# Sliding-window attention and a gated MLP in one kernel: the last store of the output in two halves on two queues

## The chip, the cores and the metric

The kernel runs on one core of a Trainium2 chip. The metric is the device time of one launch in microseconds. Several launches are timed and their median is given. One further launch is recorded by the hardware profiler, and every row of the profile comes from that one.

The engines go by short names here, as in the profile: PE multiplies matrices, ACT (ScalarE) applies functions and copies, DVE (VectorE) and POOL (GpSimd) work elementwise, and SP (SyncE) only issues transfers and waits. A letter q behind a name (ACTq, SPq) is that engine's instruction sequencer. PEld is PE loading weights.

## The reference

```python
# q, k, v: (4, 8, 768, 64); n_sink = 4, window = 128
scores = (1 / sqrt(D)) * q @ k.transpose(0, 1, 3, 2)
rel = pos[:, None] - pos[None, :]
keep = (pos[None, :] < n_sink) | ((rel >= 0) & (rel < window))
a = softmax(where(keep, scores, -1e9))
x = (a @ v).transpose(0, 2, 1, 3).reshape(3072, 512)
h = x @ w_in                       # w_in: (512, 2048)
g = h * (1 / (1 + exp(-1.702 * h)))
out = g @ w_out                    # w_out: (2048, 512), out: (3072, 512) float32
```

Each token attends to the first four positions of its sequence and to a window of 128 positions. The result, 3072 tokens by 512 features, goes through two matrix products with a gate between them.

## The kernel before

The 3072 tokens are 24 blocks of 128 (`NBLK`), and two blocks at a time make one of 12 groups (`NG`). For each block the attention is computed: loads of q, k and v, transposes, scores, exponentials, the product with v and its normalisation, up to the tile `xn`. A group then goes through the MLP: line 802 multiplies its transposed tokens `xt` by `w_in` into PSUM tiles `mm`, line 832 applies the gate on ACT and writes `gt`, and line 856 multiplies `gt` by `w_out`, sixteen accumulating matmuls for each output tile. The output tile is copied from PSUM to the SBUF tile `osb` (lines 375 to 381, by ACT or DVE), and line 874 stores it to `out_dram` in HBM.

Every output tile is 128 tokens by 512 columns and is stored whole, except the very last one (group 11, second block; `end` is true for it). It is computed in three column parts, as `CFG["last"] = (256, 128, 128)` says: each part has its own sixteen matmuls, its own copy and its own store. So the last store of the kernel is 128 rows by 128 columns of 4 bytes, 64 KB, with 512 bytes in each row.

The order of the work is written out by hand. `SEQUENCE` is a list of words such as `832a`: the number of an operation in the order in which `plan.add` made them, and the letter of the engine that is to issue it (p PE, a ACT, d DVE, t POOL, s SP). `Plan.run` reads nothing else. The numbers that `plan.add` also takes (costs, `xfer`, `post`, `slack`, the keys) are kept with the operation, and this kernel does not use them for the order. A dictionary such as `{SP: 0.5, ACT: 0.5}` says which engines may issue the operation, and `by(e)` picks the queue by the letter.

The end of the list is `831p 821a 827s 832a 833a`. Here 831 is the last quarter of the last part's matmuls, 821 the store of the first part on ACT's queue, 827 the store of the second part on SP's queue, 832 the copy of the last part on ACT, and 833 its store, on ACT's queue.

Each transfer that SP or ACT issues signals its landing on one of eight lanes (semaphores), taken in turn, and before a lane is used again the issuing queue waits until the lane's former transfer has landed. After its last transfer, SP goes through the lanes and waits for each of them. Then the engines meet and the program ends. The profile shows these last waits and the meeting under line 916.

Of the kernel before, what the change touches and what calls it, by code (L numbers as in the profile page):

```python
# [19 lines left out]
P = 128  # L20
# [3 lines left out]
NG = 12  # L24
# [3 lines left out]
PE, ACT, DVE, POOL, SP = "PE", "ACT", "DVE", "POOL", "SP"  # L28
CFG = dict(
    tq=(0, 1, 2, 3, 4, 5, 6, 7),  # L30
    ta=(0, 1, 2, 3, 4, 5),
    tx=(0, 1, 2, 3, 4, 5),
    nb={2: 1, 3: 1},
    wide={1: 'pv', 3: 'pv'},
    fine=(0, 1, 2, 3),
    split=(0, 1),
    gbatch={},
    tanh=(0, 1),
    last=(256, 128, 128),
    hw=['k0'],  # L40
    big=(0, 1, 2, 3),
# [48 lines left out]
775a 764d 766p 767a 776p 777a 780p 781a 782p 462t 754p 788p 463p 755p 464d 789p 477s 783p 647s 756p 765s 709s 784p  # L90
790p 757p 758a 785p 759s 791p 786a 787s 792d 796p 731s 797a 808p 809a 794p 795a 802p 803a 806p 807a 798p 799a 800p
801a 810p 804p 805a 811p 816p 812p 822p 813p 817p 823p 814a 818p 824p 815s 819p 793s 828p 825p 820a 829p 826a 830p
831p 821a 827s 832a 833a
"""


# [69 lines left out]
def kernel(  # L166
# [28 lines left out]
    plan = Plan(RING)  # L195
# [48 lines left out]
    def by(e):  # L244
        return nc.sync if e == SP else nc.scalar
# [24 lines left out]
    ld, qkn = {}, {}  # L270

    def load_block(which, b, key, after=0.0):
        bb, r = divmod(b, 6)
        pair, i = divmod(PLACE[b], 2)
        src = {"q": q, "k": k, "v": v}[which][bb, :, r * P : (r + 1) * P, :].rearrange("h s d -> s h d")
        if which == "v":
            return sw(key, 0.88, lambda b=b, x=2: nc.gpsimd.dma_start(v65[:, b, :, 0:D], src), 0.88 if pair < 4 else 0.95, deps=[z_1], after=after)  # L277
        w = "qk".index(which)
        buf = qkn[pair]
        if which + str(PLACE[b]) in CFG["hw"]:  # L280
            raw = const.tile([P, H * D], FP32, name=f"raw_{which}{b}")
            n = CFG["hw"].index(which + str(PLACE[b]))
            src = {"q": q, "k": k}[which][bb, :, r * P : (r + 1) * P, :].rearrange("h (t e) d -> t h (e d)", e=8)
            got = plan.add(
                {SP: 0.45, ACT: 0.6}, -120 + n, 0, lambda e, src=src, raw=raw, x=9: by(e).dma_start(raw, src), xfer=0.9, post=0.6
            )

            def round16(e, b=b, w=w, i=i):
                dst, src = buf()[:, i, w].rearrange("p h d -> p (h d)"), raw
                if e == ACT:  # L290
                    nc.scalar.copy(out=dst, in_=src)
                else:
                    (nc.vector if e == DVE else nc.gpsimd).tensor_copy(out=dst, in_=src)

            return plan.add({DVE: 0.42, ACT: 0.6, POOL: 0.8}, -110 + n, 0, round16, deps=[got], take=[buf])
        if PLACE[b] in CFG["big"]:
            return sw(
                key, 0.56,
                lambda b=b, w=w, i=i: nc.gpsimd.dma_start(
                    buf()[:, i, w].rearrange("p h d -> p (h d)"),  # L300
                    {"q": q, "k": k}["qk"[w]][bb, :, r * P : (r + 1) * P, :].rearrange("h (t e) d -> t h (e d)", e=8),
                ),
                0.7, take=[buf], after=after,
            )
        return sw(
            key, 0.88, lambda b=b, w=w, i=i: nc.gpsimd.dma_start(buf()[:, i, w], src), 0.88 if pair < 4 else 0.95,  # L306
            take=[buf], after=after,
        )
# [84 lines left out]
    for p, b in enumerate(ORDER):  # L393
# [8 lines left out]
        if p in CFG["tq"]:  # L402
            tps = [ps(t, (P, 4, P), FP16, f"tq{b}_{w}") for w, t in enumerate(CFG["tqb"][p])] if p in CFG["tqb"] else []
            tps = tps or [ps("mm", (P, 8, P), FP16, f"tq{b}")] * 2
            if p in CFG["big"]:
                tps = [
                    ps(t, (P, 4, P), FP32, f"tq{b}_{w}")
                    for w, t in enumerate(CFG["tqb"].get(p, ("mm", "mm")))
                ]

            def tp(w, tps=tps):
                return tps[w]()[:, 4 * w : 4 * w + 4] if tps[0] is tps[1] else tps[w]()

            def t_qk(w, g=g, i=i, p=p, tp=tp):
                src = qkn[g]()[:, i, w].rearrange("p h d -> p (h d)")
                if p in CFG["big"]:
                    dst = tp(w).rearrange("p c t -> p (c t)")
                    for e in range(8):
                        for a in range(2):
                            nc.tensor.matmul(  # L420
                                dst[64 * a : 64 * a + 64, 64 * e : 64 * e + 64],
                                src[:, 64 * e : 64 * e + 64],
                                ident.rearrange("p (t c a) -> p t c a", a=2, t=16)[:, :, :, a], start=True, stop=True,
                            )
                    return
                for c in range(4):
                    nc.tensor.transpose(tp(w)[:, c], src[:, bass.ts(c, P)], ident)

            def copy_qk(e, w, b=b, p=p, tp=tp):
                dst, src = qk_of(b)[:, 4 * w : 4 * w + 4], tp(w)  # L430
                if p in CFG["big"]:
                    dst, src = (
                        dst.rearrange("p c (t e) -> p c t e", e=8),
                        src.rearrange("p x y -> p (x y)").rearrange("p (e t c) -> p c t e", c=4, t=16),
                    )
                copy(e, dst, src)

            parts = []
            for w in range(2):
                a = plan.add(  # L440
                    PE, K0 - 48 + w, 0.43 if p in CFG["big"] else 0.24, lambda w=w, f=t_qk: f(w), deps=[ld["qk"[w] + str(b)], o_const],
                    take=[tps[w]], give=[qkn[g]],
                )
                parts.append(
                    plan.add(
                        {DVE: 0.6 if p in CFG["big"] else 0.34, ACT: 0.5}, K0 - 48 + w, 0,
                        lambda e, b=b, w=w, f=copy_qk: f(e, w),
                        deps=[a], take=[qkt[g]], give=[tps[w]],
                    )
                )  # L450
            o_qkt[b] = parts
        elif i == 0:

            def t_qk(g=g):
                nc.sync.dma_start_transpose(
                    qkt[g]().rearrange("p i c t -> p (i c) t"), qkn[g]().rearrange("p i w h d -> p (i w h d)")
                )

            o_qkt[b] = o_qkt[ORDER[p + 1]] = [
                plan.add(  # L460
                    SP, K0 - 48, 1.75, t_qk, deps=[ld[f"{w}{n}"] for w in "qk" for n in ORDER[p : p + 2]], take=[qkt[g]],
                    give=[qkn[g]], xfer=2.56, post=0.75,
                )
            ]
# [22 lines left out]
        def uniq(bufs):  # L487
            return list(dict.fromkeys(bufs))
# [20 lines left out]
        if r == 0:  # L509
            s_msk = plan.add(  # L510
                PE, K0 - 41, 0.45, lambda own=half, f=masks: f(own), deps=[o_const] + (o_qkt[b] if p else []), take=uniq(owns),
                slack=slack["s"],
            )
            s_own = plan.add(
                PE, K0 - 40, 0.46, lambda b=b, own=half, f=scores: f(own, b),
                deps=o_qkt[b] + [s_msk], give=[qkt[g]], use=uniq(owns),
            )
        else:

            def both(b=b, own=half, prv=prv, f=scores):  # L520
                f(own, b)
                f(lambda lo, hi: prv()[:, lo:hi], b - 1)

            s_own = plan.add(
                PE, K0 - 40, 0.57, both, deps=o_qkt[b] + o_qkt[b - 1], take=uniq(owns) + [prv],
                give=[qkt[g]] + ([qkt[PLACE[b - 1] // 2]] if PLACE[b - 1] // 2 != g else []),
                slack=slack["s"],
            )

            def sinks(b=b, bb=bb, snk=snk):  # L530
                for j in range(4):
                    nc.tensor.matmul(snk()[:, j], qk_of(b)[:, j], ksb[:, bb, j], start=True, stop=True)  # L532

            s_snk = plan.add(PE, K0 - 40, 0.1, sinks, deps=([s_own] if p >= CFG['steady'] else []) + o_qkt[b] + [o_ks[bb]], take=[snk], give=[qkt[g]], slack=slack["s"])
# [252 lines left out]
    for g in range(NG):  # L787
# [53 lines left out]
        for t in range(2):  # L841
# [4 lines left out]
            for part, width in enumerate(CFG["last"] if end else (d_model,)):  # L846
# [5 lines left out]
                for n in range(4):  # L852
# [16 lines left out]
                    ),  # L869
                    deps=[prev], take=[osb], give=[po],  # L870
                )
                plan.add(
                    {SP: 0.5, ACT: 0.5} if end else SP, 16 * g + 12 + 4 * t, 0.5,
                    lambda e=SP, row=row, osb=osb, cols=cols: by(e).dma_start(out[row : row + P, cols], osb()[:, cols]),
                    deps=[ev], give=[osb], xfer=0.72 * share, post=2.0 if g >= NG - 3 else 1.0,
                )

    order = plan.run()
    with tc.manual_schedule():
# [41 lines left out]
```

## Time and profile before

| | us |
|---|---|
| median of three runs | 227.18 |
| the three runs | 227.09, 227.18, 228.92 |
| the profiled run, as timed | 228.16 |
| span of the profiled run | 226.5 |
| PE busy in it | 214.0 (94%) |

The span runs from the first to the last instruction that the profile has. The profiled run took 1.7 us more than its span, which lie outside of what the profile shows. Its granted TensorE clock was 1.00. The profile's lines are shown in the prediction, where they are used.

### The profile page before, as it was taken

The numbers are of one execution on the slowest core, as the hardware profiler recorded it, in microseconds if no ns is written. First come the engines' busy times: TensorE is split into PE (matmuls) and PEld (weight loads), VectorE is DVE, ScalarE is ACT, GpSimd is POOL, SyncE is SP. The second block draws the span as 40 slices with busy tenths as digits, with TensorE's granted clock in tenths as the row PEclk, the third lists the DMA queues.
The fourth block names the chain that finished last, engine by engine and source line by source line (L and its number), as shares of the span: only waits on it lengthen the run. The fifth ranks groups of instructions, "written<-read, shape, count | busy, mean of one in ns | idle before, by whom it ended". The sixth has DMA issues, their size and how long they took to land.

```text
span 226.5 us, 5648 instructions
## 1 busy us (share of the span) xinstructions
PE 214.0 (94%) x2378; PEld 151.9 (67%) x2378; DVE 133.3 (59%) x238; ACT 141.6 (63%) x201; POOL 113.9 (50%) x137
## 2 busy tenths in 40 slices
PE   1977999999999999999999999999999999999994
PEld 1557876776784686684695685697764777754864
DVE  1898988689678782782886677466477371110100
ACT  2487786768859848348247559767694766812622
POOL 8592756869990399860893480763405230210000
PEclk9999999999999999999999999999999999999999
DMA  6999999999999999999999999399967620206303
GB/s 131 166 204 193 177 189 195 156 129 160 140 149 158 255 169 138 146 123 187 285 145 138 227 112 151 59 228 96 225 98 139 92 56 3 52 0 206 121 0 139
DMA packets 123512, 32.47 MB, mean 143 GB/s; under 512 B 114880, under 2 KB 120416, under 8 KB 123488
## 3 DMA queue, kind: packets, MB, share of 16 engines
q0 software_dynamic: 71792, 13.51, 74.2%
q1 hardware_dynamic: 51408, 18.42, 39.8%
q8 instruction: 18, 0.29, 0.5%
q10 hardware_dynamic: 288, 0.20, 0.3%
q14 instruction: 6, 0.05, 0.1%
HBM read 27.46 MB, written 6.29 MB: 149 GB/s over the span
## 4 chain that ended last, share of the span: by engine, by line
PE 69%; DMA 20%; POOL 5%; DVE 2%; issue 1%; SPq 1%; ACT 0%; POOLq 0%
PE mm L856 30%; PE mm L802 28%; DMA qkn<-in_q_dram 7%; DMA w_in<-in_moe_w_in_dram 4%; DMA qkt<-qkn 3%; DMA at<-a 3%; PE own L503 2%; POOL qkn L306 2%; PE av L741 2%; PE av L737 2%; PE av L731 2%; DMA consts<-cconst 2%; PE prv L503 1%; DVE e L600 1%; POOL at L646 1%
## 5 line engine op out<-in xcount | busy, mean ns | idle before, releaser
L802 PE MATMUL mm<-xt,w_in 128*128 128x256 f16 (+1 forms) x896 | 93.8, 257 | 1.8 <-DMA w_in<-in_moe_w_in_dram 1.4
L856 PE MATMUL mm<-w_out,gt 128*128 128x512 f16 (+2 forms) x416 | 91.9, 363 | 0.0
L802 PEld LDWEIGHTS <-w_in 128*128 128x128 f16 x896 | 75.2, 98 | 14.4 <-DMA w_in<-in_moe_w_in_dram 1.8
L832 ACT ACTIVATE gt<-mm 128x512 f16<-128x512 f32 x88 | 51.0, 596 | 47.4 <-PE mm L802 47.0
L856 PEld LDWEIGHTS <-gt 128*128 128x128 f16 x416 | 37.2, 98 | 32.1
L642 POOL TENSOR_SCALAR_AFFINE_SELECT atp<-at 128x1024 f16<-128x1024 f16 (+1 forms) x22 | 22.3, 1014 | 69.3 <-DMA at<-a 65.5
L549 DVE COPY_PREDICATED own<-consts,prv 128x1024 f32<-128x1024 uint16 x20 | 24.6, 1228 | 24.8 <-PE prv L503 24.8
L559 DVE TENSOR_REDUCE mx<-own 128x8 f32<-128x1024 f32 (+1 forms) x28 | 29.8, 1069 | 1.5 <-PE own L503 0.7
L600 DVE TENSOR_TENSOR e<-own,mx 128x1024 f32<-128x1024 f32 (+1 forms) x26 | 28.4, 1094 | 0.6
L639 ACT ACTIVATE a<-e 128x1056 f16<-128x1056 f32 (+1 forms) x26 | 25.0, 979 | 1.9 <-DVE e L624 1.3
L646 POOL TENSOR_SCALAR_AFFINE_SELECT at<-at 128x1024 f16<-128x1024 f16 (+1 forms) x22 | 22.5, 1024 | 1.5
L277 POOL DMA_DIRECT2D v<-in_v_dram x24 | 21.6, 906 | 1.9 <-DMA w_out<-in_moe_w_out_dram 1.9
L381 ACT COPY osb<-mm 128x512 f32<-128x512 f32 (+2 forms) x16 | 8.4, 531 | 18.8 <-PE mm L856 15.7
L306 POOL DMA_DIRECT2D qkn<-in_q_dram x20 | 17.9, 901 | 3.4 <-DMA w_in<-in_moe_w_in_dram 1.8
L832 ACT ACT_TABLE_LOAD x15 | 19.2, 1283 | 0.3
L306 POOL DMA_DIRECT2D qkn<-in_k_dram x20 | 17.8, 902 | 2.4 <-PE snk L532 1.6
L639 ACT ACT_TABLE_LOAD x14 | 18.0, 1283 | 0.2
L749 DVE TENSOR_TENSOR xn<-av,rcp 128x512 f16<-128x512 f32 (+1 forms) x25 | 16.0, 638 | 0.9
L737 PE MATMUL av<-v,at 128*128 128x65 f16 x180 | 16.1, 194 | 0.1
L748 DVE RECIPROCAL rcp<-av 128x8 f32<-128x8 f32 (+1 forms) x25 | 5.0, 199 | 18.7 <-PE av L741 18.5
L737 PEld LDWEIGHTS <-at 128*128 128x128 f16 x192 | 14.1, 97 | 2.6 <-ACT at L381 0.7
L377 DVE COPY osb<-mm 128x512 f32<-128x512 f32 x8 | 5.5, 690 | 16.8 <-PE mm L856 16.4
(67 smaller groups left out, 174.6 us busy)
## 6 DMA issues: line engine op xcount, KB each, us to landing
out_dram<-osb SPq DMA_DIRECT2D x23, 256.0 KB, 2.6
qkn<-in_q_dram POOLq DMA_DIRECT2D x24, 128.0 KB, 5.4
v<-in_v_dram POOLq DMA_DIRECT2D x24, 128.0 KB, 5.2
qkn<-in_k_dram POOLq DMA_DIRECT2D x23, 128.0 KB, 6.5
w_in<-in_moe_w_in_dram POOLq DMA_DIRECT2D x4, 512.0 KB, 9.9
w_out<-in_moe_w_out_dram POOLq DMA_DIRECT2D x4, 512.0 KB, 11.4
at<-a SPq DMA_TRANSPOSE x18, 3.5
raw_k<-in_k_dram SPq DMA_DIRECT2D x1, 256.0 KB
```

The costliest lines, as they stand in the source:

```text
L277: return sw(key, 0.88, lambda b=b, x=2: nc.gpsimd.dma_start(v65[:, b, :, 0:D], src), 0.88 if pair < 4 else 0.95, deps=[z_1], after=after)
L306: key, 0.88, lambda b=b, w=w, i=i: nc.gpsimd.dma_start(buf()[:, i, w], src), 0.88 if pair < 4 else 0.95,
L549: nc.vector.copy_predicated(out=own(lo, hi).rearrange("p l j s -> p (l j) s"), mask=later.unsqueeze(1).to_broadcast((P, 4 * (hi - lo), P)) ...
L559: lambda lo=lo, hi=hi, own=half, small=small: nc.vector.tensor_reduce(out=small[:, lo:hi], in_=own(lo, hi), axis=AX.X, op=ALU.max),
L600: nc.vector.tensor_tensor(out=e32()[:, 512 * lo : 512 * hi].rearrange("p (l j s) -> p l j s", j=4, s=P), in0=own(lo, hi), in1=small[:, lo: ...
L639: nc.scalar.activation(out=a16()[:, lo:hi], in_=e32()[:, lo:hi], func=AF.Exp, scale=scale)
L642: nc.gpsimd.affine_select(out=atp()[:, lo : lo + n], in_=at()[:, lo : lo + n], pattern=[[0, n], [-1, P]], compare_op=ALU.is_gt, fill=0.0, ...
L646: nc.gpsimd.affine_select(out=at()[:, lo : lo + n], in_=at()[:, lo : lo + n], pattern=[[0, n], [1, P]], compare_op=ALU.is_ge, fill=0.0, ba ...
L737: nc.tensor.matmul(acc[:, j], at()[:, c], v65[:, b, h], start=(r == 0), stop=(r == 0))
L802: nc.tensor.matmul(ht()[:, n], w_in16[:, c, bass.ts(f, P)], xt[g]()[:, tok, c], start=(c == 0), stop=(c == 3))
L832: lambda fs=fs, cols=cols, gt=gt, ht=ht: nc.scalar.activation(out=gt()[:, fs[0] : fs[-1] + 1, cols], in_=ht(), func=AF.Gelu_apprx_sigmoid),
L856: nc.tensor.matmul(po(), gt()[:, F, bass.ts(t, P)], w_out16[:, F, cols], start=(F == 0), stop=(F == NF - 1))
```

## The change

The store of the last part, and no other, is made in two: `pieces` is 2 for the last part of the last tile. The first piece takes rows 0 to 63 of `osb`, the second rows 64 to 127, each with the same 128 columns. Both depend on the same copy (832). The first keeps number 833 and ACT's queue; the second is the new operation 834, with the letter s, so SP issues it. All other words of `SEQUENCE` are the same.

The diff also alters four numbers that `plan.add` keeps with operations (a `post`, two costs of PE steps, and POOL as an engine that could do one rounding step). The written order does not read them.

```diff
-831p 821a 827s 832a 833a
+831p 821a 827s 832a 833a 834s
...
-                {SP: 0.45, ACT: 0.6}, -120 + n, 0, lambda e, src=src, raw=raw, x=9: by(e).dma_start(raw, src), xfer=0.9, post=0.6
+                {SP: 0.45, ACT: 0.6}, -120 + n, 0, lambda e, src=src, raw=raw, x=9: by(e).dma_start(raw, src), xfer=0.9, post=1.25
...
-            return plan.add({DVE: 0.42, ACT: 0.6, POOL: 0.8}, -110 + n, 0, round16, deps=[got], take=[buf])
+            return plan.add({DVE: 0.42, ACT: 0.6}, -110 + n, 0, round16, deps=[got], take=[buf])
...
-                    PE, K0 - 48 + w, 0.43 if p in CFG["big"] else 0.24, lambda w=w, f=t_qk: f(w), deps=[ld["qk"[w] + str(b)], o_const],
+                    PE, K0 - 48 + w, 0.40 if p in CFG["big"] else 0.24, lambda w=w, f=t_qk: f(w), deps=[ld["qk"[w] + str(b)], o_const],
...
-                PE, K0 - 40, 0.57, both, deps=o_qkt[b] + o_qkt[b - 1], take=uniq(owns) + [prv],
+                PE, K0 - 40, 0.65, both, deps=o_qkt[b] + o_qkt[b - 1], take=uniq(owns) + [prv],
...
-                plan.add(
-                    {SP: 0.5, ACT: 0.5} if end else SP, 16 * g + 12 + 4 * t, 0.5,
-                    lambda e=SP, row=row, osb=osb, cols=cols: by(e).dma_start(out[row : row + P, cols], osb()[:, cols]),
-                    deps=[ev], give=[osb], xfer=0.72 * share, post=2.0 if g >= NG - 3 else 1.0,
-                )
+                pieces = 2 if end and part == len(CFG["last"]) - 1 else 1
+                for piece in range(pieces):
+                    at_rows = slice(piece * P // pieces, (piece + 1) * P // pieces)
+                    plan.add(
+                        {SP: 0.5, ACT: 0.5} if end else SP, 16 * g + 12 + 4 * t, 0.5,
+                        lambda e=SP, row=row, osb=osb, cols=cols, rows=at_rows: by(e).dma_start(
+                            out[row + rows.start : row + rows.stop, cols], osb()[rows, cols]
+                        ),
+                        deps=[ev], give=[osb], xfer=0.72 * share / pieces, post=2.0 if g >= NG - 3 else 1.0,
+                    )
```

## The prediction

> **What bounds the kernel now.** I read the page's first part and its chain first, then the end of the chain, and then, since the change touches only the end, the timeline, the transfers and the waits of the last three microseconds.
>
> ```profile
> span 226.5 us, 5648 instructions
> PE 214.0 (94%) x2378; PEld 151.9 (67%) x2378; DVE 133.3 (59%) x238; ACT 141.6 (63%) x201; POOL 113.9 (50%) x137
> PE 69%; DMA 20%; POOL 5%; DVE 2%; issue 1%; SPq 1%; ACT 0%; POOLq 0%
> ```
>
> PE is busy for 94% of the span and carries 69% of the chain that ends last. The 20% of DMA in it are loads and transposes, and the change touches none of them. So the body of the kernel stays as it is, and the question is what happens behind the last matmul. The chain, asked from 217 us on, has this:
>
> ```profile
> 217.26 6.14 PE mm L856 x60
> 223.40 0.02 issue
> 223.42 0.27 ACT osb L381
> ```
>
> The chain ends with the last copy, at 223.42 + 0.27 = 223.69. The span ends at 226.5. The 2.8 us between them are the last store and what waits for it, and they have to be read from other views. The timeline of the two queues:
>
> ```profile
> 222.76 0.37 ACTq L874 DMA_DIRECT2D out_dram<-osb  x1
> 223.42 0.27 ACT L381 COPY osb<-mm 128x128 f32<-128x128 f32 x1 [0.40 <-PE mm L856]
> 223.72 0.34 ACTq L874 DMA_DIRECT2D out_dram<-osb  x1
> ...
> 223.05 0.33 SPq L874 DMA_DIRECT2D out_dram<-osb  x1
> ```
>
> ACT issues the last store 0.03 behind the copy, and the issue takes 0.34, to 224.06. SP issued its own last store at 223.05 and was done with that at 223.38, so it stands free 0.31 before the last copy ends. What the transfer engines then do, in 40 slices of 25 ns from 224.4 to 225.4:
>
> ```profile
> DMA  0000000547999996521000000000000000000000
> GB/s 0 0 0 0 0 0 20 164 143 246 307 348 348 348 246 185 144 62 41 21 0 0 0 0 0 0 0 0 0 0 0 0 0 0 0 0 0 0 0 0
> DMA packets 144, 0.07 MB, mean 66 GB/s; under 512 B 16, under 2 KB 144, under 8 KB 144
> q10 hardware_dynamic: 144, 0.07, 22.3%
> ```
>
> These 144 packets are the last store: 128 rows and 16 small ones, on ACT's queue (q10). The first move in the seventh slice, at 224.55, and the last in the twentieth, at 224.90. The first lie 224.55 - 223.72 = 0.83 behind the start of the issue. The 16 engines were busy for 22.3% of 1 us, which is 0.22 each, spread over 0.35 because they do not all begin together. Then the landing, from the waits of SP's queue on line 916 between 225.2 and 225.6:
>
> ```profile
> L916 SPq EVENT_SEMAPHORE  x5: 28/28/28, 225.3 to 225.6; - x5
> ...
> SPq L916 <- DMA out_dram<-osb: 0.5, 1, 0.5
> ```
>
> SP saw the last store landed at 225.3, which is 0.4 behind its last packet. Four more checks of lanes take it to 225.6, about 0.07 each, and the remaining 0.9 to the end of the span are the engines' meeting. So of the 2.8 us behind the copy, 0.83 go until packets move, 0.35 are movement, 0.4 the way from the last packet to the signal, and 1.2 the closing of the program. The change can shorten or lengthen the second of these, and the first for one half of the rows. The other terms do not depend on how the bytes are divided.
>
> **The change part by part.** The instruction lists of the two builds differ in this: ACT's last store is 64x128 in place of 128x128, SP has one store of 64x128 more at its end (69 rows in place of 68), and the line numbers behind it are shifted. The four altered numbers of the planner leave every list as it was, so their cost is nothing, and there is no cover that could go.
>
> *ACT's store with 64 rows.* Does its issue get shorter with fewer rows? The nearest rows:
>
> ```profile
> L250 SPq DMA_DIRECT2D ownm<-cown x1: 391/391/391, 41.3 to 41.3; - x1
> ...
> L874 ACTq DMA_DIRECT2D out_dram<-osb x2: 343/355/367, 222.8 to 223.7; - x2
> ```
>
> A transfer with 32 rows took 0.39 to issue and those with 128 rows 0.34 and 0.37. The issue does not follow the number of rows, so I take 0.34 for 64 rows too, and 0.83 until its first packet.
>
> *SP's new store.* It waits for the same copy. SP's queue is free 0.31 before, so it issues beside ACT, at about 223.72, and takes the 0.33 of its former store: nothing is added to the path by the issue itself. It needs a lane again, so SP first checks that lane's former transfer. By the instruction list that is the store of an earlier tile, issued in the stretch from 208 to 214, and the packets of that stretch were through by 211.4:
>
> ```profile
> DMA  0000000299992399999999300000000000000000
> out_dram<-osb SPq DMA_DIRECT2D x3, 256.0 KB, 4.5
> ```
>
> The slices here are of 0.15. The three stores in it landed, at the median, 4.5 after their issue, which is by 214, ten microseconds early. The check falls into SP's free time. Queued behind the new store on SP are its closing waits, and all engines wait for these. They begin at about 224.06 in place of 223.38. How much room they have:
>
> ```profile
> SPq L916 <- DMA out_dram<-osb: 1.7, 4, 0.6
> ```
>
> SP stood waiting for landings for 1.7 us in all in these closing waits. Until 225.3 it needs only a few checks of 0.07 each, so the 0.68 of delay lies inside these 1.7. If the cover were gone, it would cost up to 0.68.
>
> *The transfer.* The bytes are the same. A second transfer adds at most another 16 small packets. Two queues now feed the engines, each with half the rows. From below: the engines cannot do the work in less than the 0.22 that they were busy, so at the best 0.35 - 0.22 = 0.13 is won, if both halves begin together and the uneven start closes. From above: SP's half begins behind ACT's by a whole issue, 0.33. Then its packets begin at 224.55 + 0.33 = 224.88 and need half of 0.22 and the same spread of 0.13, to 225.12, which is 0.22 later than 224.90 (an estimate from these rows). Between -0.13 and +0.22 I take 0.0: both queues begin 0.83 behind an issue that starts at the same time, the bytes are the same and I assume that the engines share them as before, and the unevenness of the start (0.13), which belongs to how the engines are set off and not to the bytes, probably stays.
>
> A rule of the Trainium skill speaks against the change. The page "DMA: Bandwidth & Descriptors", section "Rules for kernel authors", says of two transfers to disjoint partition halves: don't bother, they serialize, because both halves use the same 16 engines. By it the lower bound falls away and the sum is 0.0 with no -0.13 beside it. The row with 22.3% agrees that the engines are the common part, and it leaves the 0.13 open.
>
> *The sum.* Span 226.5 + 0 (issue) + 0 (closing waits) + 0.0 (transfer, -0.13 to +0.22) = 226.5. The profiled run took 228.16, 1.7 more than its span. The median of the three runs is 227.18, and the same sum on it gives 227.2.
>
> **The rivals.** *One issue at a time.* ACT's and SP's issues use something in common, and the second waits for the first. Against it: SP's row at 223.05 began while ACT's (222.76 + 0.37 = 223.13) still ran. They overlapped by 0.08, and SP's took 0.33, no longer than the ACT issue that ran alone (0.34). For it: 0.08 of 0.33 is a small overlap, and the change makes it complete. The time: +0.22 as worked out, 227.4. It decides once SP's packets begin later than ACT's by more than the 0.11 of busy time that a half takes.
>
> The Trainium skill has this as a rule: "Perfetto Trace Analysis", section "DMA Instruction — HWDGE (DVE, Sync)", says that the block which makes the descriptors is shared between the issuing sequencers and is locked for exclusive use by one instruction. The time by it is the +0.22 above. The overlap of 0.08 without a longer issue speaks against a lock over the whole issue, not against one over a part of it.
>
> *The even start.* Two queues set the engines off more evenly and the 0.13 is won: 227.05. For it: the digits rise over five slices before they reach 9. Against it: the same digits would rise so if the engines are started one after the other whatever the queue.
>
> *A slow landing.* SP's half, as the second of two stores in flight, lands as late as the three stores from 208 to 214, 4.5 after its issue. Then SP sees it at 223.72 + 4.5 = 228.2 in place of 225.3, +2.9, and the median would be 230.1. It passes 1% (2.27 us) if that landing takes more than 1.6 + 2.27 = 3.9, where the last store of before had 1.6:
>
> ```profile
> DMA to landing us min/median/max: 1.6/1.6/1.6
> ```
>
> Against it: those three were of 256 KB each, and here are two of 32 KB. The two stores that were in flight together at the end of before had landed by the same closing waits, none of which lasted over 0.6.
>
> That the change does not do what it says is ruled out by the lists.
>
> **How the numbers follow.** The forecast, no change to speak of (within 0.1), has 0.60; one issue at a time 0.22; the even start 0.14; the slow landing 0.02; 0.02 is left for a measurement that strays. The time is that of the likeliest, 227.2. About 1% is what a measurement of this kernel can tell from no change. Nothing here reaches a gain of 1%, so faster gets 0.01 for a stray measurement. Slower gets 0.03, from the slow landing and the other half of the stray ones. Within 1% is left with 0.96. The cases reach from 227.05 to 227.4. The runs themselves scatter more: 227.09 to 228.92, with the profiled one at 228.16, so a median of a few runs can well come out as high as 228.2. Downwards I take the lowest run less the 0.13, 226.96, and 0.3 below it, since three runs show the lower end only roughly. The range is 226.7 to 228.2.
>
> **What would show it.** In the profile after, two issues of line 877 should begin within 0.05 of each other, some 0.03 behind the last copy, each about 0.33 long. If SP's takes 0.5 or more, the issues go one at a time. The two queues' packets (q10 and q1, 80 each at most) should both begin about 0.83 behind the issues and end about 0.35 later; an end at 0.22 shows the even start. The last landing should stand 1.6 behind the issue, and 1.2 should follow until the end of the span. PE's busy time and the chain up to the last copy should be those of before. I am wrong if the part from the copy's end to the end of the span is not 2.8 within 0.2, or if the body of the kernel moves although no instruction in it changed.

## The result, and the profile after

| | before | after |
|---|---|---|
| median of 22 runs | 227.76 us | 228.49 us |
| lowest and highest | 226.86, 228.92 | 227.55, 229.82 |
| ratio after to before | | 1.0032 (95% interval 1.0017 to 1.0046) |
| the profiled run, as timed | 228.16 us | 228.24 us |

The changed kernel is slower by 0.3%, which is 0.7 us (0.4 to 1.05 by the interval). The kernel before came out at 227.76 over 22 runs, where the three runs shown at first had 227.18.

The page and the end of the chain of waits, after:

```profile
span 226.5 us, 5650 instructions
PE 213.9 (94%) x2378; PEld 151.9 (67%) x2378; DVE 133.0 (59%) x238; ACT 141.5 (62%) x201; POOL 113.9 (50%) x137
...
216.84 6.14 PE mm L856 x60
222.97 0.02 issue
223.00 0.27 ACT osb L381
```

The span is 226.5 as before, and it would be wrong to read from that that nothing happened. The last copy ends at 223.27 where it ended at 223.69 before. The body of this execution was 0.4 shorter, and the end took back as much. The body scatters: over the executions recorded in this study, all with the same instructions up to the last copy or nearly so, the last copy began between 222.2 and 225.5. Against this, the distance from the last copy's end to the end of the span is almost fixed for one kernel. It is called the tail from here on, and is taken from the trace's time stamps, which are in nanoseconds: 2.77 before, 3.26 after. The tail grew by 0.49.

Where, is seen in the last issues of the two queues (the timeline, asked for each engine by itself), in the transfers from 224.4 to 225.4 in slices of 25 ns, and in SP's waits:

```profile
223.00 0.27 ACT L381 COPY osb<-mm 128x128 f32<-128x128 f32 x1 [0.40 <-PE mm L856]
223.29 0.55 ACTq L877 DMA_DIRECT2D out_dram<-osb  x1
...
223.29 0.56 SPq L877 DMA_DIRECT2D out_dram<-osb  x1
```

```profile
DMA  0000235798999974421000000000000000000000
GB/s 0 0 0 0 82 82 143 205 266 246 307 308 267 247 185 103 103 42 21 20 0 0 0 0 0 0 0 0 0 0 0 0 0 0 0 0 0 0 0 0
DMA packets 160, 0.07 MB, mean 66 GB/s; under 512 B 32, under 2 KB 160, under 8 KB 160
q10 hardware_dynamic: 80, 0.03, 12.3%
q1 hardware_dynamic: 80, 0.03, 11.7%
```

```profile
L921 SPq EVENT_SEMAPHORE  x5: 28/28/28, 225.3 to 225.6; - x5
...
SPq L921 <- DMA out_dram<-osb: 0.9, 1, 0.9
```

The two issues begin together, as intended, but each takes 0.55 in place of 0.34. The first packet moves at 224.50, 1.21 behind the issue in place of 0.85 (the prediction read 0.83 from slices of 25 ns; by the time stamps it is 0.85). The movement takes 0.4. SP's last long wait, for ACT's landing, is 0.9 in place of 0.5, and the landing of its own half lets it pass 0.17 after that. By the time stamps the tail's growth divides into 0.37 until ACT's first packet, 0.06 in the movement and 0.12 between the last packet and SP's seeing it. After the landing SP goes through one lane fewer, which takes 0.07 off.

### The profile page after: what moved, and what is told of

The parts are those of the page before. It is cut to its first block, busy times and chain, and to the rows that moved or that the text cites. A ratio compares the mean times of both kernels' runs of the same rounds, so it can differ in the third digit from the quotient of the medians.

```text
span 226.5 us, 5650 instructions
## 1 busy us (share of the span) xinstructions
PE 213.9 (94%) x2378; PEld 151.9 (67%) x2378; DVE 133.0 (59%) x238; ACT 141.5 (62%) x201; POOL 113.9 (50%) x137
## 4 chain that ended last, share of the span: by engine, by line
PE 86%; DMA 10%; DVE 1%; issue 0%; SPq 0%; POOL 0%; ACT 0%
PE mm L856 37%; PE mm L802 35%; DMA qkn<-in_q_dram 4%; DMA w_in<-in_moe_w_in_dram 4%; PE own L503 3%; PE av L741 2%; PE av L737 2%; PE av L731 2%; PE prv L503 2%; DMA consts<-cconst 2%; PE snk L532 1%; PE mm L427 1%; DVE e L600 1%; DVE mx L559 1%; PE mm L679 1%; PE own L495 0%
```

## The experiments

The end of every execution is read in the same way. All times in this table are in us, from the trace's time stamps. "Lag" is from the start of the issue to the first packet, "landing" from the last packet to SP's passing its wait for the last landing. Where two stores end the kernel, ACT's stands first.

| kernel | last stores | issue | lag | landing | tail |
|---|---|---|---|---|---|
| before | 128 rows | 0.34 | 0.85 | 0.41 | 2.77 |
| after | 64 rows and 64 rows | 0.55, 0.56 | 1.21, 1.28 | 0.53 | 3.26 |
| after, once more | the same | 0.55, 0.56 | 1.21, 1.27 | 0.53 | 3.27 |
| half of the rows alone | 64 rows | 0.53 | 1.19 | 0.36 | 3.03 |
| half of the columns alone | 128 short rows | 0.34 | 0.85 | 0.38 | 2.67 |
| column halves | 128 and 128 short rows | 0.37, 0.33 | 0.94, 0.83 | 0.55 | 2.95 |
| 96 and 32 rows | 96 rows and 32 rows | 0.38, 0.34 | 0.89, 0.84 | 0.43 | 2.83 |

**One half alone.** Is it the second issue that makes the first slow, or the form of the store? The most direct test keeps ACT's half and drops SP's.

```diff
-831p 821a 827s 832a 833a 834s
+831p 821a 827s 832a 833a
...
-                for piece in range(pieces):
+                for piece in range(1):
```

> Rows 64 to 127 of the last part are not stored; ACT stores rows 0 to 63 alone. Theory A (two issues at the same time hinder each other): with no issue beside it, ACT's takes 0.34 again, not 0.55, its packets begin 0.85 behind its start, and the end of the span comes 2.7 to 2.8 behind the last copy, as before the change. Theory B (a store of 64 rows is slow by itself): ACT's issue takes 0.55 although it is alone, and the end comes 3.2 behind the copy. Theory C (the cost is a second landing to wait for): 0.55 for the issue remains, but the end comes 0.1 to 0.2 earlier than after the change, as SP's later landing is gone.

```profile
223.35 0.27 ACT L381 COPY osb<-mm 128x128 f32<-128x128 f32 x1 [0.40 <-PE mm L856]
223.65 0.53 ACTq L877 DMA_DIRECT2D out_dram<-osb  x1
```

With nothing beside it, the issue of 64 rows still takes 0.53. Theory A has fallen for the issue, theory B holds for it. But the tail is 3.03, between the 2.77 of before and the 3.26 of the change, so something is left that the second store brings: 0.23, where theory C had said 0.1 to 0.2. The time was 1.0007 of the kernel before (0.9975 to 1.0038), which does not tell 0.26 us from none.

**Both halves on ACT's queue.**

```diff
-831p 821a 827s 832a 833a 834s
+831p 821a 827s 832a 833a 834a
```

> Both halves are issued by ACT, one behind the other. Theory A: the issues cannot overlap, so each takes about 0.34, the second begins 0.38 behind the first, its packets begin 0.85 behind that, and the end comes about 2.8 + 0.38 - 0.1 = 3.1 behind the copy, near the 3.2 of the change although only one queue is used. Theory B: each takes 0.55, and the end comes about 3.6 behind the copy. Theory C: each 0.34, and the end 3.1 or later, because two landings are waited for.

```profile
L877 ACTq DMA_DIRECT2D out_dram<-osb x2: 522/568/614, 225.8 to 226.3; - x2
```

The issues took 0.52 and 0.61, one behind the other, and the tail was 3.61: theory B's numbers. The landing of the second was seen 0.37 behind its last packet, as for a store alone. The ratio was 1.0094 (1.0057 to 1.0131) from four runs, more than the 0.84 us in the tail account for (0.4%). The last copy of its profiled run ended 2.1 us later than in before and 2.5 later than in after. Why these four were slower is not settled.

**The halves one after the other on two queues.** The last copy is cut in two as well, and ACT stores the first half before it copies the second.

```diff
-831p 821a 827s 832a 833a 834s
+831p 821a 827s 832a 833a 834a 835s
...
+                for piece in range(2 if last else 1):
+                    at_rows = slice(64 * piece, 64 * piece + 64) if last else slice(0, P)
...
-                        e, osb()[:, cols], po(), 0.5 if x in CFG["tanh"] else 1.0
+                            e, osb()[rows, cols], po()[rows], 0.5 if x in CFG["tanh"] else 1.0
```

> The last copy is made in two halves of 64 rows with ACT's store of the first between them, so SP issues the second half about 0.65 behind ACT. Theory A: no overlap, both issues take 0.33 to 0.34, and SP's packets begin 0.85 behind its issue; from the second copy's end to the end of the span 2.7 to 2.8, the amount from before. Theory B: both issues take 0.55, and the end comes 3.1 or later behind the second copy. Theory C: issues of 0.34, the first half has long landed, and the end comes 2.8 behind the second copy; together with the single store this would leave A and C to be told apart by the issue times in the other runs.

```profile
222.76 0.53 ACTq L877 DMA_DIRECT2D out_dram<-osb  x1
223.33 0.26 ACT L381 COPY osb<-mm 64x128 f32<-64x128 f32 x1 [0.60 <-ACT osb L381]
...
223.62 0.56 SPq L877 DMA_DIRECT2D out_dram<-osb  x1
```

No overlap, and still 0.53 on ACT and 0.56 on SP: the form is slow on either queue. From the second copy's end to the end of the span it took 2.99, near the 3.03 of a half alone (theory B had said 3.1 or later). The time was 1.0056 of the kernel before (1.0038 to 1.0073): the whole copy would have ended 0.86 earlier, and with the 0.22 of the longer tail that makes 1.08 us, 0.5%.

**Halves by columns.** The same two queues at the same time and the same bytes, but all 128 rows in each store.

```diff
-                    at_rows = slice(piece * P // pieces, (piece + 1) * P // pieces)
+                    at_rows = slice(0, P)
+                    step = (whole.stop - whole.start) // pieces
+                    cols = slice(whole.start + piece * step, whole.start + (piece + 1) * step)
```

> The last part is split by columns in place of rows: 128 rows of 256 bytes on each of ACT's and SP's queues at the same time. Theory A with a price for each row (the queues share the making of descriptors): twice the rows of the change, so each issue takes about 0.34 + 0.44 = 0.78, and the end comes 3.6 or later behind the copy. Theory A with a price for each transfer: 0.55 each as in the change, and the end about 3.3 behind the copy. Theory B (64 rows are slow): 0.34 each, since the rows are 128, and the end 2.8 behind the copy. Theory C: 0.55 or less each, and the end 3.0 to 3.2.

```profile
L880 SPq DMA_DIRECT2D out_dram<-osb x1: 332/332/332, 222.5 to 222.5; - x1
L880 ACTq DMA_DIRECT2D out_dram<-osb x1: 365/365/365, 222.5 to 222.5; - x1
```

Two issues that begin 4 ns apart take 0.33 and 0.37. So a simultaneous issue makes an issue 0.03 longer at most, and the 0.2 of the change belongs to 64 rows. ACT's first packet does come 0.09 later beside another issue (0.94 in place of 0.85), so a small part may be shared. The tail was 2.95 and not the 2.8 that theory B alone gave. The ratio was 1.0005 (0.9977 to 1.0034).

**Half of the columns alone** gives the fourth corner: the same edit, made on the kernel with the column halves.

```diff
-831p 821a 827s 832a 833a 834s
+831p 821a 827s 832a 833a
...
-                for piece in range(pieces):
+                for piece in range(1):
```

> Columns 64 to 127 of the last part are not stored; ACT stores the other 64 columns, 128 rows of 256 bytes, alone. It is the fourth corner beside the single half of 64 rows (3.0 from the copy's end to the end of the span), the pair of those (3.3) and the pair of column halves (2.9). If a pair costs 0.2 whatever its form, the end comes 2.7 behind the copy, and the packets begin 0.85 behind the issue in place of 0.94. If the pair of column halves costs nothing by itself, it comes 2.9 behind.

```profile
224.50 0.27 ACT L381 COPY osb<-mm 128x128 f32<-128x128 f32 x1 [0.40 <-PE mm L856]
224.80 0.34 ACTq L880 DMA_DIRECT2D out_dram<-osb  x1
```

The tail was 2.67. The four corners now add up. From the whole store to half its bytes: 2.77 to 2.67, 0.1 won. From 128 short rows to 64 long ones: 2.67 to 3.03, 0.36 lost. From one such store to two: 3.03 to 3.26, 0.23 lost; by columns 2.67 to 2.95, 0.28 lost. The larger part of the second store's price is in the landing: in the pairs SP saw the last landing 0.53 and 0.55 behind the last packet, in the single stores 0.36 and 0.38, a difference of 0.17 each time. Another 0.13 (rows) and 0.11 (columns) passes before the last packet. With the row halves SP then goes through one lane fewer, which takes 0.07 off.

**Which numbers of rows are slow?** A ladder of stores in SP's idle time, in the kernel before: parts of a tile that is already stored are stored again, one behind the other.

```diff
+LADDER = ((0, 128, 0, 128), (0, 64, 128, 256), (0, 96, 256, 384), (64, 96, 128, 256), (96, 112, 128, 256), (64, 128, 384, 512), (0, 64, 384, 512), (96, 128, 256, 384))
...
+    for lo, hi, left, right in LADDER:
+        plan.add(
+            SP, 900, 0.5,
+            lambda row=row, osb=osb, lo=lo, hi=hi, cols=slice(left, right): nc.sync.dma_start(
+                out[row + lo : row + hi, cols], osb()[lo:hi, cols]
+            ),
+            deps=[stored], give=[osb],
+        )
```

> The kernel before, with eight more stores on SP's queue in its idle time before the last tile's: parts of a tile that is already stored are stored again, of 128, 64, 96, 32, 16, 64, 64 and 32 rows of 512 bytes, one behind the other. Stores one behind the other took 0.42 to 0.46 to issue with 128 rows in the trace of before. Theory D1 (any number of rows other than 128 takes a slower way, a fixed 0.18 more): all but the first take 0.60 to 0.65. Theory D2 (the price grows as the rows get fewer): 96 rows 0.50, 64 rows 0.62, 32 rows 0.7, 16 rows 0.75. Theory D3 (a form that the queue has not just had costs once): each change of form 0.6, the second of the two neighbouring stores of 64 rows 0.44. The time stays that of before.

In their order, the issues took 0.33 (128 rows), 0.57 (64), 0.57 (96), 0.42 (32), 0.42 (16), 0.52 (64), 0.59 (64) and 0.58 (32). None of the three theories gives this row: 32 rows come out both ways. What it leaves open is whether a store was slow by itself or because of the one ahead of it on the queue. So the next two kernels let each store of such a ladder wait for the landing of the one before, by making them overlap.

```diff
-LADDER = ((0, 128, 0, 128), (0, 64, 128, 256), (0, 96, 256, 384), (64, 96, 128, 256), (96, 112, 128, 256), (64, 128, 384, 512), (0, 64, 384, 512), (96, 128, 256, 384))
+LADDER = ((0, 64, 0, 128), (0, 32, 0, 128), (0, 96, 0, 128), (0, 128, 0, 128))
...
+LADDER = ((0, 16, 0, 128), (0, 112, 0, 128), (64, 128, 0, 512), (0, 128, 0, 512))
```

> The kernel before, with four more stores in SP's idle time, of parts of a tile that is already stored: 64, 32, 96 and 128 rows of 512 bytes. They overlap, so each waits for the landing of the one before and is issued alone, as the last store of the kernel is. Theory D1 (any number other than 128 is slow): 0.53, 0.53, 0.53 and 0.33. Theory D2 (fewer rows, slower): 32 rows above 64, 64 above 96, 128 at 0.33. Theory D4 (64 and 96 rows are slow, few rows are not, as the ladder has it but for its last store): 0.53, 0.33, 0.50 and 0.33. The packets of 64 rows begin 1.2 behind the issue, those of 128 rows 0.85. As in the kernel with four more stores, the end comes 2.5 behind the last copy.

> The same with 16 rows and 112 rows of 512 bytes, 64 rows of 2048 bytes and 128 rows of 2048 bytes. D1: 0.53, 0.53, 0.53 and 0.33. D2: 16 rows slowest, 112 near 0.36. D4: 0.33, 0.50, 0.53 and 0.33. If the length of a row decides as well, the 64 rows of 2048 bytes differ from the 0.53 that 64 rows of 512 bytes took. End 2.5 behind the last copy.

The timeline of SP's queue, one row asked for each store (64, 32, 96 and 128 rows in the first kernel; 16, 112, 64 and 128 in the second):

```profile
213.44 0.57 SPq L885 DMA_DIRECT2D out_dram<-osb  x1
215.35 0.35 SPq L885 DMA_DIRECT2D out_dram<-osb  x1
216.78 0.32 SPq L885 DMA_DIRECT2D out_dram<-osb  x1
218.30 0.35 SPq L885 DMA_DIRECT2D out_dram<-osb  x1
```

```profile
214.94 0.34 SPq L885 DMA_DIRECT2D out_dram<-osb  x1
216.37 0.32 SPq L885 DMA_DIRECT2D out_dram<-osb  x1
217.93 0.57 SPq L885 DMA_DIRECT2D out_dram<-osb  x1
220.27 0.36 SPq L885 DMA_DIRECT2D out_dram<-osb  x1
```

Only 64 rows are slow: 0.57, with rows of 512 bytes and of 2048, in the lower and in the upper half, first in the row or third. 16, 32, 96, 112 and 128 rows take 0.32 to 0.36. The lags agree: 1.22 for both stores of 64 rows, 0.82 to 0.86 for all others. Theories D1, D2 and D4 have all fallen. The ladder is explained with it: the stores of 96 and 32 rows that took 0.57 and 0.58 stood right behind one of 64 rows, the two of 32 and 16 rows that took 0.42 did not. What stands right ahead on the queue matters for 128 rows too: in the kernel before, SP's stores of 128 rows took 0.57 to 0.65 right behind a transposing transfer (`DMA_TRANSPOSE`), 0.42 to 0.46 right behind another plain transfer, and else 0.33 to 0.38. So only issues made with nothing right ahead can be compared.

**The change with another cut.** If this is the cause, the change loses most of its price when one number in it is altered.

```diff
-                    at_rows = slice(piece * P // pieces, (piece + 1) * P // pieces)
+                    at_rows = slice((0, 96)[piece], (96, 128)[piece]) if pieces == 2 else slice(0, P)
```

> The change with one number altered: ACT stores rows 0 to 95 and SP rows 96 to 127, both at the same time, in place of 64 and 64. Theory E (64 rows, and only they, cost 0.2 in the issue and 0.35 until the first packet; two stores that end together cost 0.25 more whatever their form): both issues 0.32 to 0.37, first packets 0.82 to 0.95 behind them, and the end 2.9 to 3.0 behind the last copy, between the 2.8 of before and the 3.3 of the change; the time is 0.1% above the kernel before, which five rounds may not tell from none. Theory D1 (any number but 128 is slow): issues of 0.53 and the end at 3.2 to 3.3. If two stores cost nothing once neither has 64 rows, the end is at 2.8 or earlier.

```profile
L877 SPq DMA_DIRECT2D out_dram<-osb x1: 343/343/343, 224.7 to 224.7; - x1
L877 ACTq DMA_DIRECT2D out_dram<-osb x1: 375/375/375, 224.7 to 224.7; - x1
```

The issues are back at 0.34 and 0.38, and the tail is 2.83, a little better than the 2.9 to 3.0 expected. The second store costs less here, and the landing is 0.43: SP's 32 rows were through 0.16 before ACT's 96, where the two equal halves ended within 0.03 of each other, and the column halves within 0.12. The ratio to the kernel before was 1.0014 (0.9991 to 1.0038).

**The change once more.**

> The changed kernel once more, for a second reading of its end on this chip. If the end's lengthening is the form of the store and not chance: both issues 0.55 to 0.57, the first packets 1.2 behind them, and the end 3.2 to 3.3 behind the last copy. If it was chance, one of the three is back at 0.34, 0.85 or 2.8.

Issues of 0.55 and 0.56, lags of 1.21 and 1.27, a tail of 3.27, and a ratio of 1.0033 (1.0008 to 1.0058). It was not chance.

**A shorter tail.** Reading the closing waits suggested another thing. SP goes through its eight lanes in a fixed order, and behind the last store's lane four more stood. With four more transfers ahead of it, the last store takes the last lane. First by four redundant stores in SP's idle time (the ladder with four times 128 rows), then without redundancy, by issuing an earlier tile's store in five parts by columns.

```diff
+LADDER = ((0, 128, 0, 128), (0, 128, 128, 256), (0, 128, 256, 384), (0, 128, 384, 512))
```

> The kernel before, with four more stores of 128 rows in SP's idle time, so that the last store's lane is the last that SP checks. In the trace of before four more checks of 0.06 each followed the landing of the last store. If these stand on the path, the end comes 0.24 earlier: 2.5 behind the last copy in place of 2.8, and the time would be 0.1% below the kernel before, about what five rounds can just tell or not. If they do not, 2.8.

```diff
-                    lambda e=SP, row=row, osb=osb, cols=cols: by(e).dma_start(out[row : row + P, cols], osb()[:, cols]),
+                    lambda e=SP, row=row, osb=osb, cols=slice(0, 256) if five else cols: by(e).dma_start(
+                        out[row : row + P, cols], osb()[:, cols]
+                    ),
...
+    for left in range(256, 512, 64):
+        plan.add(
+            SP, 900, 0.5,
+            lambda row=row, osb=osb, cols=slice(left, left + 64): nc.sync.dma_start(out[row : row + P, cols], osb()[:, cols]),
+            deps=[ev], give=[osb],
+        )
```

> The kernel before, with the store of one earlier tile, in SP's idle time, issued in five parts by columns (256 and four times 64, always 128 rows), so that no byte is stored twice and the last store's lane is the last one checked. If the order of the checks is the cause of the earlier end in the kernel with four more stores, the end comes 2.5 behind the last copy here too and the time is 0.1% below the kernel before. If the redundant stores did it in another way, 2.8 and no gain.

The wait for the last landing, in the kernel with five parts, between 225.85 and 226.05:

```profile
L929 SPq EVENT_SEMAPHORE  x1: 28/28/28, 225.9 to 225.9; - x1
```

It is one wait where before had five between 225.3 and 225.6. The tails were 2.52 and 2.53 (and 2.55 in both kernels with the spaced stores, which also have four more), 0.24 to 0.25 below the 2.77 of before. The ladder of eight stores is the control: eight more go once round the eight lanes, so the last store keeps the lane it had, and its tail is 2.78. In the time this is 0.1%: ratios of 0.9984 (0.9963 to 1.0005) and 0.9990 (0.9963 to 1.0017). Both point downwards, and neither tells a gain from none.

## Why the prediction was wrong

*What bounds the kernel, and that only the tail can move.* Right as far as the runs show. Where kernels with the same end were recorded more than once, their tails agree within 0.03; the tail's growth of 0.49 lies inside the measured 0.4 to 1.05, and the kernels that change the tail's terms move it. That the rest of the measured 0.7 is scatter of the body is inferred, not shown, and the kernel with both halves on ACT's queue was slower than its tail accounts for, which stays open. The prediction named its own sign of being wrong, a tail that is not 2.8 within 0.2, and the tail came out at 3.26.

*"The issue does not follow the number of rows, so I take 0.34 for 64 rows too, and 0.83 until its first packet."* This is the step that failed. It went from rows of 32 and 128 to 64 between them, and 64 is the one number tried that is slow: 0.52 to 0.57 for the issue and 1.2 until the first packet, alone or beside another. The term that the sum put at nothing, "0 (issue)", measured 0.36. With the 0.23 of the second store, less the 0.10 that half the bytes save, that makes the 0.49. The row of 32 rows with its 0.39 was also no like case: it was a load, and SP issued it 0.05 after its issue before; a store of 32 rows alone took 0.35.

*"The other terms do not depend on how the bytes are divided."* Wrong too, and the smaller part. With two stores that end together SP saw the last landing 0.53 behind the last packet in place of 0.36 to 0.41. The second store cost 0.23 in the tail, most of it there.

*The transfer, -0.13 to +0.22, taken as 0.0.* The movement itself took 0.4 in place of 0.35, inside the bounds. Half the bytes in one store are worth 0.1, as the single column half shows, and a pair does not get it.

*SP's issue beside ACT's, the lane and the closing waits.* Right: SP issued 0.005 from ACT, the lane was free, and no closing wait but the landings' became longer.

*The rival "one issue at a time".* It named the sign of the result and a price of +0.22, but as the prediction had it, with the second issue waiting for the whole of the first, it is refuted: two issues 4 ns apart took 0.33 and 0.37 once neither had 64 rows. The test it was given, SP's issue taking 0.5 or more, came true for another reason, since both took as long. The Trainium skill's rule behind it ("Perfetto Trace Analysis", section "DMA Instruction — HWDGE (DVE, Sync)"), that the block is locked for one instruction, shows no such price here: a lock over the whole issue would have made one of the two 0.66 (an estimate from 0.33 twice). A lock over a small part is not excluded: one of the two was 0.03 longer, and its first packet came 0.09 later.

*The other rivals.* The even start did not come. The slow landing of 4.5 did not come either; the landings stood 2.0 to 2.2 behind the issue.

*The rule against the change.* The Trainium skill, "DMA: Bandwidth & Descriptors", section "Rules for kernel authors", advises against two transfers to disjoint partition halves because they share the engines. The result agrees with the advice. That the engines are shared would explain that nothing was gained; the loss came from the form of 64 rows and from the second store, mostly its landing, which that rule does not name.

*The range.* It was set about the median of three runs, 227.18, and its upper end of 228.2 was meant to hold the scatter. Over 22 runs the kernel before itself stood at 227.76. With the 0.7 on top the result passed the end by 0.3. The same 0.7 on 227.18 would have stayed inside, so the range missed by its base as much as by the step that failed.

## What to carry to other kernels

When the total scatters by more than an edit can be worth, measure the stretch that the edit touches (here from the last copy to the end of the span), which repeated within 0.03 and gave an answer where twelve runs gave none. A cost between two measured shapes is not safe to interpolate: issue the very shape once in an idle stretch of the queue, alone and not right behind another, and read it. And the shortest tail here had one last transfer, in a shape that was read to be quick, on the lane that is waited for last; what that lane saves, 0.25 us, the times could not tell from none.

## What the runs showed of the hardware that was not expected

- A store of 64 rows from SBUF to HBM, issued by ACT or SP with nothing right ahead of it on the queue, took 0.52 to 0.57 to issue and 1.18 to 1.28 until its first packet. Those of 16, 32, 96, 112 and 128 rows took 0.32 to 0.38 and 0.82 to 0.94. It also held up the next store on its queue: 96 rows took 0.57 right behind it and 0.32 alone. Why 64 is special stays open, and no run here looked into it; numbers of rows other than these six were not tried.
- Two stores on two queues that ended together were seen to have landed 0.53 to 0.55 behind the last packet, single ones 0.36 to 0.41; with ends 0.16 apart it was 0.43. A landing is signalled in sixteen steps. In the changed kernel ACT's sixteen came from 225.06 to 225.25 and SP's from 225.24 to 225.42, although their last packets were only 0.03 apart, so the two landings were signalled one behind the other. Why is open.
- Each lane that SP waits through after the last landing costs 0.06, even when its transfers landed long before.
